# A fused long-convolution and gated-linear backward: net pace, fixed spectra homes, dW stores on another queue, four row blocks at once

## The chip, the core and the metric

One core of a Trainium2 chip runs the whole kernel in one launch. The metric is the device time of a launch in microseconds (us). The core has five engines, each with its own in-order instruction queue: TensorE (PE, matmuls), VectorE (DVE), ScalarE (ACT), GpSimd (POOL) and SyncE (SP). SP, ACT and POOL issue DMA transfers; an instruction that waits holds up everything behind it on its queue. Matmuls write to PSUM, which VectorE and ScalarE read out.

## The reference

The forward function takes the layer norm of x, multiplies a long convolution of it by a gated bilinear network, and adds x. The kernel returns its output and the gradients of everything but B_x. S = 2048 rows, D = 1024 columns, F = 3584; all tensors are bf16.

```python
xn = layernorm(x)                                 # x = A_q
k_shift = sum over t of k_pad[:, t:t+S] * shift_k[:, 3-t]
kv = k_shift * v
y = irfft(rfft(kv padded to 2S) * rfft(ssm_k padded to 2S))[:S] + kv * ssm_D
s = xn * y
h = (xn @ w_gate) * (xn @ w_up)
out = x + s * silu(h @ w_down)
_out, _vjp = jax.vjp(f, q, k, v, shift_k, ssm_k, ssm_D, w_gate, w_up, w_down)
return (out, *_vjp(grad_out))
```

## The kernel before

F is cut into 14 slabs of 256 columns (`NSL`), S into 16 row blocks of 128, D into 8 channel blocks (`ds`) of 128. The phases follow each other on TensorE; the two convolutions run beside them.

1. **Front end and gate/up** (0 to 562 us). The layer norm goes chunk by chunk over x (`ln_load`, `layer_norm`), the first two slabs of w_gate and w_up are multiplied as chunks come (`gu_unit`), and then the other slabs one after another. A tick is eight matmuls (L604). The products h are turned (`tr` L624, `hT`) and stored to HTd, Hd and GUd.
2. **Forward convolution**, beside it. `conv_forward` is a generator; `tick` calls a pump that advances it until its yielded units match the share of ticks that are done. Its spectra come from small DFT matmuls (`fwd4_half`, psF L232), whose results ACT copies and DVE combines. `shift` forms kv from k and v, which `load_kv` loads on POOL's queue, and `fwd4_half` reads kv. The spectra of kv and of ssm_k are stored to HFd and KFd.
3. **h @ w_down, gate and dbm** (562 to 755 us).
4. **dh and the weight gradients** (755 to 1379 us). Per slab `dw_slab` makes dW_gate and dW_up over eight `dc` steps (L1208), ACT casts each (L1213) into `wb` (three buffers, one per two steps), and two stores per `wb` go out on ACT's queue (`sta`). Between the steps `dh_half` computes dh of the next slab (L1191), DVE multiplies it into U, and SP stores that to DGd. `gu_in` and `load_wdt` load GUd and w_down, also on SP.
5. **Convolution backward**, beside it, pumped in the same way. `dy_forward` transforms dy (`fwd8_half`, psF; then `fwd8`) and stores DYFd; then 16 units multiply a spectrum A (DYFd) by a spectrum B (HFd or KFd), `product`, and transform back, `inv8` (psY L428).
6. **dW_down** (1379 to 1583 us): 14 steps `k`, each of two halves `f` (L1314); ACT casts into `wbs` (L1316, four buffers), SP stores it. Transposing DMAs on SP (`load_wgu` L1272 for the weights, `load_dgut` L1279 for the gradients of gate and up) run ahead for the next phase.
7. **dx** (1583 to 1991 us). dx_n is a sum over 14 pieces n, each a weight piece WGU[n] times a gradient piece dgut[n] of four row blocks (g); `dx_part` makes 8 matmuls (L1337) for one row block and n. Row blocks go in pairs; three PSUM tiles `psx` are in use. The layer norm's backward of a row block (`ln_backward`) loads dxna_t, xn_t and dout_t on SP, adds psx and dxna_t on DVE into `dxn`, and stores dx. Beside it run `dk_units` (dk and the shift gradients), 16 units paced by `kpump`, which load `kT` and `dkT` by transposing DMAs on SP and `dkh` on POOL.

What sets the order: the framework orders instructions on each engine by program order and priority, `tc.issue_after` holds an instruction behind another, and `high_priority` lifts one. `st` and `cld` issue on POOL's queue, `ld` on SP's, `sta` on ACT's. A tile of a pool waits until the last user of its buffer is done.

Of the kernel before, what the change touches and what calls it, by code (L numbers as in the profile page):

```python
# [19 lines left out]
def build_kernel(  # L20
# [217 lines left out]

    def fwd4_half(x, i, wp, psp, first=None):

        SP = wp.tile([P, 2, 2, 512], F32, name="SP", bufs=2)
        for par in range(2):
            ps = psp.tile([P, 2, 2, 256], F32, name="psF")
            cmm(ps[:, 0], T4[par], x, (i, i + 4), first if i == 0 else None, True)
            cmm(ps[:, 1], T4[par], x, (i + 2, i + 6))
            nc.scalar.copy(out=SP[:, :, par], in_=ps[:].rearrange("p s k x -> p s (k x)"))  # L246
        return SP
# [28 lines left out]
    def fwd8_half(x, i, wp, psp):  # L276

        SP = wp.tile([P, 2, 2, 512], F32, name="SP", bufs=2)
        for j in range(2):
            r = 2 * i + j  # L280
            ps = psp.tile([P, 2, 2, 256], F32, name="psF")
            cmm(ps[:, 0], T4[0], x, (r,))
            cmm(ps[:, 1], T4[0], x, (r + 4,))
            nc.scalar.copy(out=SP[:, :, j], in_=ps[:].rearrange("p s k x -> p s (k x)"))
        return SP
# [346 lines left out]
    def conv_forward():  # L632
# [39 lines left out]
        def h_rows(ds):  # L672
            hrow = S_.pop(("h", ds))
            hx = cs.tile([P, NB, P], BF16, name="hx")
            for c in range(2):
                ps = ps_tr.tile([P, 8, P], BF16, name="tr")
                with tc.issue_after(tr_ln[0].ins):
                    nc.tensor.transpose(ps[:, 0, :], hrow[:, c, :, 0], ident[:])
                for r in range(1, 8):
                    nc.tensor.transpose(ps[:, r, :], hrow[:, c, :, r], ident[:])  # L680
                nc.scalar.activation(hx[:, 8 * c:8 * c + 8, :], ps[:], ACT.Copy, scale=WSC)
            h_out.append(ds)
            if ds + 1 < 8:
                load_h(ds + 1)
            S_["hx"] = hx
# [4 lines left out]
        def tail(ds):  # L690
            G = S_.pop(("G", ds))
            yf = cs.tile([P, NB, P], BF16, name="yf")
            for rp in range(4):
                ps = inv_rows(G, ps_y, rp)
                nc.scalar.copy(out=by_res(yf[:], rp), in_=rowps(ps))
# [5 lines left out]
        load_kv(0, 0)  # L701
        load_kv(0, 1)
# [6 lines left out]
        for ds in range(8):  # L709
# [6 lines left out]
            yield 2.4  # L716
# [3 lines left out]
            yield 2.4  # L720
# [3 lines left out]
            yield 2.4  # L724
# [3 lines left out]
            yield 2.4  # L728
            W = fwd4_buf(cs)
            for i in range(2):  # L730
                fwd4_sums(W, sph[i], i)
                next(tl, None)
                yield 2.4
# [3 lines left out]
            for i in range(2):  # L737
                fwd4_outs(HX, W, i)
                next(tl, None)
                yield 2.4  # L740
# [21 lines left out]
    F_TOTAL = 4 * 20.0 + 6.0 + 8 * (0.5 + FWD4_W + 1.3 + PROD_W + INV_W) + 10.0  # L762
# [3 lines left out]
    ln_load(*xs[0])  # L766
    slabs = [load_slab(0, nc.sync)[0]]
    for c in xs[1:3]:
        ln_load(*c)
# [12 lines left out]
    last, root, xst = layer_norm(*xs[0])  # L782
    for i, (b0, n, x4) in enumerate(xs):
        if i + 1 < len(xs):
            with tc.issue_after(last.ins):
                last, root, xst = layer_norm(*xs[i + 1])
        for i_, sl in ([(i, 0), (i, 1)] if i < 4 else ([(4, 0)], [(5, 0), (4, 1), (5, 1)])[i - 4]):
# [86 lines left out]
    def dy_forward(cx, cs):  # L874
        def load(ds):
            if ds < 8:
                x = cx.tile([P, NB, P], BF16, name="dyx")
                cld(x[:], DYd[ds])
                xs_.append(x)
        xs_, sp = [], []  # L880

        def half(ds, i):
            if ds < 8:
                sp.append(fwd8_half(xs_[ds], i, cs, ps_c3))
# [5 lines left out]
        for ds in range(8):  # L890
            SPs = sp[2 * ds:2 * ds + 2]
            load(ds + 2)
            X = cs.tile([P, 16, 256], BF16, name="DX")
            yield from fwd8(SPs, X, cs, lambda i: half(ds + 1, i))
            st(DYFd[ds], X[:])

    def conv_backward():
        cx = pool("d_cx", 2)
        cs = pool("d_cs", 1)
        yield from dy_forward(cx, cs)  # L900
        ps_c3.release()
        ps_y4.append(pool("ps_y4", 4, space=PSUM))
        cs.release()
        cx.release()
        tfp.release()
        ab = pool("e_ab", 1)
        cs = pool("e_cs", 1)
        ew = pool("e_ew", 1)
# [3 lines left out]
        def load_a(n):  # L912
            if n < 16:
                As[n] = ab.tile([P, 16, 256], BF16, name="A", bufs=2)
                cld(As[n][:], DYFd[units[n][1]])

        def load_b(n):
            if n < 16:
                Bs[n] = ab.tile([P, 16, 256], BF16, name="B", bufs=2)
                cld(Bs[n][:], units[n][2][units[n][1]])  # L920
# [28 lines left out]
        PINQ[0] = False  # L949
        load_a(0)  # L950
        load_b(0)
        PINQ[0] = True
# [8 lines left out]
        ab.release()  # L961

# [241 lines left out]
    def dw_slab(sl, dgus, others):  # L1204
        for dc in range(DC):
# [123 lines left out]
    ps_x = pool("ps_x", 3, space=PSUM)  # L1329
# [136 lines left out]
```

## Time and profile before

Six runs took between 2002.84 and 2016.09 us, median 2007.62. The profiled execution is one of these.

| what | value |
|---|---|
| profiled execution, its own time | 2002.84 us |
| its span on the core | 2000.2 us |
| granted TensorE clock, mean | 0.992 |
| VectorE busy | 1512.6 us (76%) |
| ScalarE busy | 648.6 us (32%) |
| DMA traffic | 443.37 MB, mean 222 GB/s |
| packets under 512 B | 282624 of 455167 |
| matmuls, gate/up (L604) | 411.6 us, 1792 of 128x512 |
| matmuls, dW (L1208) | 397.2 us, 1792 of 128x512 |
| matmuls, dx (L1337) | 337.9 us busy for 1536 recorded |
| first dx matmul | 1591.38 us |
| last dx matmul | 1989.9 us |

Busy time is a share of the whole span and mixes phases with different limits. The wait lists give, for an engine, the line that waited, what released it, the total in us, how often, and the longest. The chain of waits, followed back from the last instruction, is on TensorE for 66% of the span, on DMA for 6% and on VectorE for 6%.

### The profile page before, as it was taken

What the parts mean: (1) busy time and instruction counts of PE and PEld (TensorE: products, weight loads), DVE (VectorE), ACT (ScalarE), POOL (GpSimd) and SP (SyncE); (2) the same over time, 40 slices, a digit from 0 to 9 for tenths busy, and PEclk for the clock granted to TensorE, in tenths of its full rate; (3) what the DMA queues carried; (4) which work ended last, traced back from release to release, by engine and by line L of the source; (5) the groups of instructions that cost most, each with busy time, mean ns of one, the idle gap of its engine ahead of it and who ended that gap; (6) DMA issues with size and microseconds to landing.
All of it is one profiled execution on the core that took longest, in us unless ns stands there. A gap on an engine that the chain in (4) does not pass through costs nothing.

```text
span 2000.2 us, 27457 instructions
## 1 busy us (share of the span) xinstructions
PE 1945.3 (97%) x11084; PEld 1044.2 (52%) x11084; DVE 1512.6 (76%) x1687; ACT 648.6 (32%) x954; POOL 331.6 (17%) x478
## 2 busy tenths in 40 slices
PE   7999999999999999999999999999999889999998
PEld 4455555555544446665566666654444334444443
DVE  7789999999636555888799999999976216666662
ACT  4765555545432224342222222222222101111112
POOL 3322213211212220000022121111212000101000
PEclk9999999999999999999999999999999999999999
DMA  8776766657799989664778898575998999696941
GB/s 287 241 265 223 252 205 228 202 178 250 255 286 295 296 268 286 210 217 171 253 238 280 207 262 268 196 279 180 210 244 184 150 222 202 149 205 145 210 113 57
DMA packets 455167, 443.37 MB, mean 222 GB/s; under 512 B 282624, under 2 KB 370488, under 8 KB 441216
## 3 DMA queue, kind: packets, MB, share of 16 engines
q1 hardware_dynamic: 367424, 226.83, 45.2%
q0 software_dynamic: 40832, 170.74, 26.3%
q10 hardware_dynamic: 46784, 44.05, 6.6%
q8 instruction: 86, 1.41, 0.3%
q14 instruction: 41, 0.34, 0.1%
HBM read 192.96 MB, written 189.83 MB: 191 GB/s over the span
## 4 chain that ended last, share of the span: by engine, by line
PE 66%; issue 15%; DVE 6%; DMA 6%; POOL 4%; SPq 2%; ACT 1%; POOLq 0%; DVEq 0%; ACTq 0%
PE psx L1337 17%; PE psb L1208 17%; PE psg L604 10%; PE psb L1314 8%; PE psb L1191 8%; PE psF L232 3%; DVE U L210 2%; SPq L1272 1%; DVE W L210 1%; DMA U<-Hd 1%; DMA KSLd<-in_A_k_dram 1%; PE psY L439 1%; DMA B<-HFd 1%; DMA dyx<-DYd 1%; PE psY L428 1%
## 5 line engine op out<-in xcount | busy, mean ns | idle before, releaser
L604 PE MATMUL psg<-wslab,U 128*128 128x512 bf16 x1792 | 411.6, 381 | 1.2 <-ACT U L570 1.1
L1208 PE MATMUL psb<-U,U 128*128 128x512 bf16 x1792 | 397.2, 379 | 0.0
L1337 PE MATMUL psx<-U,dgut 128*128 128x512 bf16 x1536 | 337.9, 382 | 15.4 <-DMA dgut<-DGd 7.8
L1337 PEld LDWEIGHTS <-dgut 128*128 128x128 bf16 x1792 | 175.7, 98 | 231.3 <-issue 12.6
L1208 PEld LDWEIGHTS <-U 128*128 128x128 bf16 x1792 | 175.2, 98 | 197.9
L604 PEld LDWEIGHTS <-U 128*128 128x128 bf16 x1792 | 173.5, 98 | 189.7 <-issue 6.3
L1191 PE MATMUL psb<-wdt,U 128*128 128x256 bf16 x1792 | 205.8, 273 | 1.1 <-ACT bm L1078 1.1
L1314 PE MATMUL psb<-U,U 128*128 128x512 bf16 x896 | 194.5, 379 | 1.8 <-DMA U<-Hd 1.8
L1191 PEld LDWEIGHTS <-U 128*128 128x128 bf16 x1792 | 175.3, 98 | 31.8 <-issue 1.4
L606 ACT CAST gut<-psg 128x512 bf16<-128x512 f32 x216 | 126.4, 586 | 180.5 <-PE psg L604 174.7
L1060 PE MATMUL psbm<-U,ht 128*128 128x512 bf16 x784 | 169.9, 379 | 0.0
L1213 ACT CAST wb<-psb 128x512 bf16<-128x512 f32 x112 | 65.6, 586 | 308.9 <-PE psb L1208 302.3
L210 DVE TENSOR_TENSOR W<-W 128x1024 f32<-128x1024 f32 (+1 forms) x144 | 142.5, 1008 | 2.9
L1314 PEld LDWEIGHTS <-U 128*128 128x128 bf16 x896 | 87.4, 98 | 106.6 <-DMA U<-Hd 2.3
L1360 ACT ACTIVATE dx_t<-dxn 128x1024 bf16<-128x1024 f32 (+1 forms) x17 | 17.1, 1007 | 334.2 <-DVE dxn L210 246.2
L1060 PEld LDWEIGHTS <-ht 128*128 128x128 bf16 x784 | 76.6, 98 | 91.8
L210 DVE TENSOR_TENSOR W<-SP 128x1024 f32<-128x1024 f32 x96 | 111.9, 1219 | 10.0 <-ACT SP L246 4.4
L1193 ACT CAST dht<-psb 128x512 bf16<-128x512 f32 x112 | 65.7, 587 | 119.1 <-PE psb L1191 113.0
L1039 DVE SCALAR_TENSOR_TENSOR dkp<-dkT,kT 128x1024 bf16<-128x1024 bf16 (+2 forms) x64 | 78.3, 1224 | 33.9 <-DMA dkT<-DKSHd 32.0
L210 DVE TENSOR_TENSOR U<-U,dht 128x2048 bf16<-128x2048 bf16 x56 | 68.3, 1221 | 44.6 <-ACT dht L1193 44.4
L210 DVE TENSOR_TENSOR m<-A,B 128x2048 bf16<-128x2048 bf16 (+1 forms) x48 | 73.1, 1575 | 31.2 <-DMA B<-HFd 16.7
L210 DVE TENSOR_TENSOR dxn<-psx,dxna_t 128x1024 f32<-128x1024 f32 (+1 forms) x17 | 19.7, 1161 | 97.6 <-DMA dxna_t<-DXNAd 63.5
(205 smaller groups left out, 2283.5 us busy)
## 6 DMA issues: line engine op xcount, KB each, us to landing
U<-GUd SPq DMA_DIRECT2D x28, 1024.0 KB, 8.1
DGd<-U SPq DMA_DIRECT2D x28, 1024.0 KB, 5.5
GUd<-gut ACTq DMA_DIRECT2D x54, 512.0 KB, 5.0
A<-DYFd POOLq DMA_DIRECT2D x16, 1024.0 KB, 8.8
out_dram<-wb ACTq DMA_DIRECT2D x112, 128.0 KB, 4.7
U<-Hd SPq DMA_DIRECT2D x14, 1024.0 KB, 6.6
Hd<-hN POOLq DMA_DIRECT2D x54, 256.0 KB, 4.3
HTd<-hT POOLq DMA_DIRECT2D x54, 256.0 KB, 3.2
```

The source lines that it names most:

```text
L210: pinned(V.tensor_tensor(o, a, b, op))
L232: mm = nc.tensor.matmul(ps[:, k].rearrange("p (c d) -> p c d", c=2), T[:, r, k, :], xr[:, r], start=(n == 0), stop=(n == len(rs) - 1 and ( ...
L604: gu_mm[0] = nc.tensor.matmul(ps[:], XNT[q][:, dc, qi * P:(qi + 1) * P], w[:, dc].rearrange("p a f -> p (a f)"), start=(dc == 0), stop=(dc ...
L606: nc.scalar.copy(out=gut[:, :, i], in_=ps[:].rearrange("p (a f) -> p a f", a=2))
L1039: ins = V.scalar_tensor_tensor(prod[:].rearrange("p r d -> p (r d)")[:, lo:H], dkT[:, 0, lo:H], 1.0, kT[:, 0, 13 + m + lo:13 + m + H], op0 ...
L1060: nc.tensor.matmul(ps[:, dh * 512:(dh + 1) * 512], ht(fc)[:, i * P:(i + 1) * P], WD[fc // 4][:, fc % 4, dh * 512:(dh + 1) * 512], start=(f ...
L1191: nc.tensor.matmul(ps[:, x * SLW:(x + 1) * SLW], DBMT[2 * hf + g][:, dc, (b % 4) * P:(b % 4 + 1) * P], wdt[:, dc, :], start=(dc == 0), sto ...
L1193: nc.scalar.copy(out=dht[:, 2 * e:2 * e + 2].rearrange("p b f -> p (b f)"), in_=ps[:])
L1208: nc.tensor.matmul(ps[:], XN[b // 4][:, b % 4, dc * P:(dc + 1) * P], dgus[b // 8][:, :, b % 8], start=(b == 0), stop=(b == NB - 1))
L1213: nc.scalar.copy(out=wb[:, dc % 2].rearrange("p a f -> p (a f)"), in_=ps[:])
L1314: nc.tensor.matmul(ps[:], h[:, b, f * P:(f + 1) * P], DBM[b // 4][:, b % 4, dh * 512:(dh + 1) * 512], start=(b == 0), stop=(b == NB - 1))
L1337: nc.tensor.matmul(ps[:, dh * 512:(dh + 1) * 512], t[n][:, f, i * P:(i + 1) * P], WGU[n][:, f, dh * 512:(dh + 1) * 512], start=(n == 0 and ...
```

## The change

Six edits are made together.

- The front end loads x's second chunk before the first slab, and the first k and v loads are held behind the store of the fifth chunk of xn (`xsts[4]`).
- The forward convolution counts the time its own matmuls take (`pe_us`), and `net` takes 0.95 of it off what a unit yields; F_TOTAL is lowered by the same sum.
- The convolution backward allots its buffers once: two homes for A (TF and A1), two for B. dy_forward's inputs and its DFT results live in A1, B0 and B1, and the first A and B are loaded in place of the half transforms that its last block has not.
- The dW_gate and dW_up stores move from ACT's queue to SP's.
- In the dW_down phase the transposing loads start one step later, and of the weight pieces 7 and of the gradient pieces 6 are issued there, not 9 and 9.
- In the dx phase four psx tiles are used. The first group g = 0 takes its four row blocks at once: for each n from 0 to 11 all four, then n = 12 and 13 for one row block after another with its ln_backward. The other groups are as before.

```diff
--- before.py
+++ after.py
@@ -236,8 +236,16 @@
             if first is not None and k == 0:
                 nc.tensor.matmul(ps[:, 0, 0:P], wsc_row[:], first, start=False, stop=True)
 
+    pe_us = [0.0]
+
+    def net(w):
+        w -= 0.95 * pe_us[0]
+        pe_us[0] = 0.0
+        return w
+
     def fwd4_half(x, i, wp, psp, first=None):
 
+        pe_us[0] += 1.75
         SP = wp.tile([P, 2, 2, 512], F32, name="SP", bufs=2)
         for par in range(2):
             ps = psp.tile([P, 2, 2, 256], F32, name="psF")
@@ -273,16 +281,14 @@
         if PIN[0]:
             tc.keep_in_program_order(ins)
 
-    def fwd8_half(x, i, wp, psp):
-
-        SP = wp.tile([P, 2, 2, 512], F32, name="SP", bufs=2)
+    def fwd8_half(x, i, SP, psp):
+
         for j in range(2):
             r = 2 * i + j
             ps = psp.tile([P, 2, 2, 256], F32, name="psF")
             cmm(ps[:, 0], T4[0], x, (r,))
             cmm(ps[:, 1], T4[0], x, (r + 4,))
             nc.scalar.copy(out=SP[:, :, j], in_=ps[:].rearrange("p s k x -> p s (k x)"))
-        return SP
 
     def fwd8(SPs, X, wp, ahead):
 
@@ -672,6 +678,7 @@
         def h_rows(ds):
             hrow = S_.pop(("h", ds))
             hx = cs.tile([P, NB, P], BF16, name="hx")
+            pe_us[0] += 0.95
             for c in range(2):
                 ps = ps_tr.tile([P, 8, P], BF16, name="tr")
                 with tc.issue_after(tr_ln[0].ins):
@@ -692,14 +699,16 @@
             yf = cs.tile([P, NB, P], BF16, name="yf")
             for rp in range(4):
                 ps = inv_rows(G, ps_y, rp)
+                pe_us[0] += 0.9
                 nc.scalar.copy(out=by_res(yf[:], rp), in_=rowps(ps))
                 if rp == 3:
                     st(YFd[:, :, ds * P:(ds + 1) * P], yf[:])
                 yield
 
         load_h(0)
-        load_kv(0, 0)
-        load_kv(0, 1)
+        with tc.issue_after(xsts[4].ins):
+            load_kv(0, 0)
+            load_kv(0, 1)
         yield from shift(0)
         PIN[0] = True
         yield 6.0
@@ -713,31 +722,31 @@
             W = fwd4_buf(cs)
             fwd4_sums(W, sp[0], 0)
-            yield 2.4
+            yield net(2.4)
...
@@ -759,14 +768,14 @@
         cs.release()
         cx.release()
 
-    F_TOTAL = 4 * 20.0 + 6.0 + 8 * (0.5 + FWD4_W + 1.3 + PROD_W + INV_W) + 10.0
+    F_TOTAL = 4 * 20.0 + 6.0 + 8 * (0.5 + FWD4_W + 1.3 + PROD_W + INV_W) + 10.0 - 0.95 * 8 * (4 * 1.75 + 0.95 + 4 * 0.9)
     chunks = [(0, 1), (1, 1), (2, 2), (4, 4), (8, 4), (12, 4)]
     xs = [(b0, n, u8((4, 6, 7)[b0 // 4 - 1], a=4) if n == 4 else lnp.tile([P, n, D], BF16, name=f"x{b0}")[:])
           for (b0, n) in chunks]
-    ln_load(*xs[0])
+    for c in xs[0:2]:
+        ln_load(*c)
     slabs = [load_slab(0, nc.sync)[0]]
-    for c in xs[1:3]:
-        ln_load(*c)
+    ln_load(*xs[2])
     slabs.append(load_slab(1, nc.sync)[0])
     for c in xs[3:]:
         ln_load(*c)
@@ -780,10 +789,12 @@
     bcast = load_bcast(bsb, ps_st)
     ang = angles(tg)
     last, root, xst = layer_norm(*xs[0])
+    xsts = [xst]
     for i, (b0, n, x4) in enumerate(xs):
         if i + 1 < len(xs):
             with tc.issue_after(last.ins):
                 last, root, xst = layer_norm(*xs[i + 1])
+            xsts.append(xst)
         for i_, sl in ([(i, 0), (i, 1)] if i < 4 else ([(4, 0)], [(5, 0), (4, 1), (5, 1)])[i - 4]):
             gu_unit(sl, *xs[i_][0:2], slabs[sl], nop)
             if i_ in (3, 4):
@@ -871,53 +882,46 @@
     ddo = const.tile([P, 8], BF16, name="ddo")
     dsko = const.tile([P, 8, 4], BF16, name="dsko")
 
-    def dy_forward(cx, cs):
+    def dy_forward(xs_, sp, cs, then):
         def load(ds):
             if ds < 8:
-                x = cx.tile([P, NB, P], BF16, name="dyx")
-                cld(x[:], DYd[ds])
-                xs_.append(x)
-        xs_, sp = [], []
+                cld(xs_[ds % 2], DYd[ds])
 
         def half(ds, i):
             if ds < 8:
-                sp.append(fwd8_half(xs_[ds], i, cs, ps_c3))
+                fwd8_half(xs_[ds % 2], i, sp[i], ps_c3)
+            else:
+                then[i]()
         load(0)
         load(1)
         yield 4.0
         half(0, 0)
         half(0, 1)
         for ds in range(8):
-            SPs = sp[2 * ds:2 * ds + 2]
             load(ds + 2)
             X = cs.tile([P, 16, 256], BF16, name="DX")
-            yield from fwd8(SPs, X, cs, lambda i: half(ds + 1, i))
+            yield from fwd8(sp, X, cs, lambda i: half(ds + 1, i))
             st(DYFd[ds], X[:])
 
     def conv_backward():
-        cx = pool("d_cx", 2)
+        ab = pool("e_ab", 1)
+        flat = lambda t, pat: t[:].rearrange(pat)
+        A_ = [flat(TF, "p a r k f -> p (a r k f)")] + [flat(ab.tile([P, 16, 256], BF16, name="A1"), "p a x -> p (a x)")]
+        B_ = [flat(ab.tile([P, 16, 256], BF16, name=f"B{i}"), "p a x -> p (a x)") for i in range(2)]
+        spec = lambda t: t.rearrange("p (a x) -> p a x", a=16)
         cs = pool("d_cs", 1)
-        yield from dy_forward(cx, cs)
-        ps_c3.release()
-        ps_y4.append(pool("ps_y4", 4, space=PSUM))
-        cs.release()
-        cx.release()
-        tfp.release()
-        ab = pool("e_ab", 1)
-        cs = pool("e_cs", 1)
-        ew = pool("e_ew", 1)
         units = [("v", ds, HFd) for ds in range(8)] + [("h", ds, KFd) for ds in range(8)]
         As, Bs, side_in = {}, {}, {}
 
         def load_a(n):
             if n < 16:
-                As[n] = ab.tile([P, 16, 256], BF16, name="A", bufs=2)
-                cld(As[n][:], DYFd[units[n][1]])
+                As[n] = spec(A_[n % 2])
+                cld(As[n], DYFd[units[n][1]])
 
         def load_b(n):
             if n < 16:
-                Bs[n] = ab.tile([P, 16, 256], BF16, name="B", bufs=2)
-                cld(Bs[n][:], units[n][2][units[n][1]])
+                Bs[n] = spec(B_[n % 2])
+                cld(Bs[n], units[n][2][units[n][1]])
 
         def load_side(n):
             kind, ds, _ = units[n]
@@ -946,10 +950,14 @@
                 return dkv_tail(ds, Bs[n], side_in.pop(n), ew)
             return dh_tail(ds, Bs[n], ew)
 
-        PINQ[0] = False
-        load_a(0)
-        load_b(0)
-        PINQ[0] = True
+        yield from dy_forward([A_[1][:, 2048 * i:2048 * i + 2048].rearrange("p (b d) -> p b d", b=NB) for i in range(2)],
+                              [b_.bitcast(F32).rearrange("p (s j x) -> p s j x", s=2, j=2) for b_ in B_], cs,
+                              (lambda: load_b(0), lambda: load_a(0)))
+        ps_c3.release()
+        ps_y4.append(pool("ps_y4", 4, space=PSUM))
+        cs.release()
+        cs = pool("e_cs", 1)
+        ew = pool("e_ew", 1)
         tl = None
         for n in range(16):
             yield from staggered(main(n), tl, 7.0)
@@ -959,6 +967,7 @@
         ew.release()
         cs.release()
         ab.release()
+        tfp.release()
 
     def dkv_tail(ds, G, tiles, ew):
         v, ksh = tiles
@@ -1214,7 +1223,7 @@
             if dc % 2 == 1:
                 fs, rows = slice(sl * SLW, (sl + 1) * SLW), slice((dc - 1) * P, (dc + 1) * P)
                 for a, dst in enumerate((o_dwg, o_dwu)):
-                    sta(dst[rows, fs].rearrange("(c p) f -> p c f", p=P), wb[:, :, a])
+                    ld(dst[rows, fs].rearrange("(c p) f -> p c f", p=P), wb[:, :, a])
             after_group(2)
             next(others, None)
 
@@ -1285,10 +1294,10 @@
         if k + 2 < NSL:
             load_h(k + 2)
         with tc.issue_after(wst.ins) if k > 0 else nullcontext():
-            if k in (1, 2, 3, 4, 5):
-                load_wgu(k - 1, u8((7, 0, 1, 9, 2)[k - 1], a=4))
-            if k in (6, 7, 8, 9):
-                ts.append(load_dgut(0, k - 6))
+            if k in (2, 3, 4, 5, 6):
+                load_wgu(k - 2, u8((7, 0, 1, 9, 2)[k - 2], a=4))
+            if k in (7, 8, 9, 10):
+                ts.append(load_dgut(0, k - 7))
         if k == 11:
 
             bdrain()
@@ -1296,15 +1305,12 @@
             tip.release()
             gw = pool("gw", 1)
             gd = pool("gd", 1)
-            for i in range(2):
-                load_wgu(5 + i, gw.tile([P, 4, D], BF16, name=f"W{i}")[:])
+            load_wgu(5, gw.tile([P, 4, D], BF16, name="W0")[:])
+        if k == 12:
+            load_wgu(6, gw.tile([P, 4, D], BF16, name="W1")[:])
             ts.append(load_dgut(0, 4))
-        if k == 12:
-            load_wgu(7, u8(6, a=4))
-            ts += [load_dgut(0, n) for n in (5, 6)]
         if k == 13:
-            load_wgu(8, u8(3, a=4))
-            ts += [load_dgut(0, n) for n in (7, 8)]
+            ts.append(load_dgut(0, 5))
         h = hs.pop(k)
         for f in range(2):
             wbs = wo.tile([P, D], BF16, name="wbs")[:]
@@ -1326,7 +1332,7 @@
     gl = pool("gl", 2, side="right")
     gs = pool("gs", 4, side="right")
     kw_ = pool("kw", 1)
-    ps_x = pool("ps_x", 3, space=PSUM)
+    ps_x = pool("ps_x", 4, space=PSUM)
     PIN[0] = True
     kpump, kdrain = make_pump(dk_units(kw_), DK_TOTAL)
     kcnt = [0]
@@ -1370,11 +1376,26 @@
             pinned(V.scalar_tensor_tensor(dx_t[:, cl], dxn[:, cl], RSTN[:, b:b + 1], dout_t[:, cl], op0=MUL, op1=ADD))
             (st if parts == 1 else ld)(out_1.flatten_outer_dims()[rows, cl], dx_t[:, cl])
 
-    for i, j in enumerate((11, 10, 8, 4, 5)):
+    for n in range(6, 14):
         with tc.issue_after(wst.ins):
-            load_wgu(9 + i, u8(j, a=4))
-            ts.append(load_dgut(0, 9 + i))
-    for g in range(4):
+            if n > 6:
+                load_wgu(n, u8((6, 3, 11, 10, 8, 4, 5)[n - 7], a=4))
+            ts.append(load_dgut(0, n))
+    pss = [ps_x.tile([P, D], F32, name="psx") for i in range(4)]
+    pss = pss[2:] + pss[:2]
+    for n in range(12):
+        for i in range(4):
+            dx_part(ts, i, pss[i], n)
+        ts[n] = load_dgut(1, n)
+    for i in range(4):
+        for n in (12, 13):
+            dx_part(ts, i, pss[i], n)
+        if i == 3:
+            for n in (12, 13):
+                ts[n] = load_dgut(1, n)
+        with tc.high_priority(40):
+            ln_backward(i, lambda h: pss[i][:])
+    for g in range(1, 4):
         for b in (4 * g, 4 * g + 2):
             if b == NB - 2:
                 break
```

More of the change, by code (lines that the diff above doesn't have):

```diff
@@ L719, in conv_forward @@
             sph = [fwd4_half(S_["hx"], 0, cs, ps_cv, D0)]
-            yield 2.4
+            yield net(2.4)
             KX = cx.tile([P, 16, 256], BF16, name="KX")
@@ L723, in conv_forward @@
             sph.append(fwd4_half(S_["hx"], 1, cs, ps_cv, D0))
-            yield 2.4
+            yield net(2.4)
             fwd4_outs(KX, W, 1)
@@ L727, in conv_forward @@
             next(tl, None)
-            yield 2.4
+            yield net(2.4)
             W = fwd4_buf(cs)
@@ L732, in conv_forward @@
                 next(tl, None)
-                yield 2.4
+                yield net(2.4)
             if ds < 7:
@@ L739, in conv_forward @@
                 next(tl, None)
-                yield 2.4
+                yield net(2.4)
             turned(HX, 1, 0, 1)
```

## The prediction

> **What bounds the kernel now.** I read the page's first part (busy us, share, instructions), then the list of waits of TensorE (PE), then the granted clock around each long wait, then the DMA-issuing queue of SyncE (SP).
>
> ```profile
> PE 1945.3 (97%) x11084; PEld 1044.2 (52%) x11084; DVE 1512.6 (76%) x1687; ACT 648.6 (32%) x954; POOL 331.6 (17%) x478
> ```
>
> TensorE is busy for 1945.3 of 2000.2 us, so all idle time is 54.9 us. No change that keeps the matmuls can win more, apart from matmuls that run slowly after a wait. The waits say where that time lies (total, times, longest):
>
> ```profile
> PE psx L1337 <- DMA dgut<-DGd: 7.8, 5, 3.1
> PE psx L1337 <- ACT wbs L1316: 7.6, 1, 7.6
> PE psF L232 <- DVE kv L210: 6.1, 3, 2.2
> PE psY L428 <- DVE B L272: 4.7, 2, 3.8
> PE tr L624 <- ACT hT L625: 4.2, 2, 3.1
> PE psb L1314 <- DMA U<-Hd: 1.8, 1, 1.8
> ```
>
> Rows 1 and 2 are at the start of the last phase, the others one each in the forward convolution, its backward, the front end and the dW_down phase. After some waits the clock drops, which the windows show (busy time of PE, PEld, DVE, ACT, POOL; then clock, DMA share, GB/s):
>
> ```profile
> 205.00:210.00 5.00, 4.72 (x28) 3.45 (x27) 4.96 (x5) 2.53 (x4) 2.80 (x4) 0.66 0.96 341
> 319.00:324.00 5.00, 4.50 (x38) 3.56 (x38) 4.96 (x5) 3.23 (x4) 1.71 (x3) 1.00 0.95 317
> 430.00:435.00 5.00, 4.60 (x26) 3.33 (x26) 4.96 (x5) 2.51 (x3) 1.38 (x3) 0.66 0.58 210
> 42.00:47.00 5.00, 5.00 (x31) 2.52 (x31) 2.46 (x8) 4.00 (x6) 4.83 (x7) 0.66 0.56 170
> 993.00:999.00 6.00, 4.11 (x20) 2.54 (x20) 5.96 (x8) 2.34 (x4) 0.00 (x0) 0.72 0.30 115
> 1591.00:1596.00 5.00, 4.62 (x13) 1.69 (x13) 4.66 (x7) 0.33 (x1) 0.00 (x0) 0.58 0.03 11
> ```
>
> A clock of 0.66 over 5 us is 0.34 x 5 = 1.7 us of work lost beside the wait.
>
> **Part by part, on the profiled run's clock (2002.84 us, 2.6 us around its span).**
>
> *Front end.* POOL issues in order. It waits for the KSLd copy (11.47 to 30.34, in the chain of waits), because load_kv's k load stands there; hT's stores stand behind it, and one starting at 34.43 takes 7.11 us to land. That gives the 3.05-us wait at 41.99 (row 5), then 1.7 us at the low clock. After, load_kv follows the fifth chunk's XNd store (49.46), so hT's stores go at once: 4.75 us gained. A later transposition then waits some 0.3 us longer (my estimate from 1.56 us at 49.22). k and v now land near 63 (issue 52 to 58, landing about 5 us); the shift's first product is at 64.13, so the cover is about 1 us, and if it is gone the DVE queue slips and PE with it later. Loading x's second chunk before slab 0 removes 0.53 us of DVE wait and delays slab 0 by about 0.4 us: nil. Take **-4.5** (-5 to 0).
>
> *Net pace.* The pump advances the convolution per tick of eight matmuls (1.73 us). F_TOTAL falls by 0.95 x 8 x 11.55 = 87.8 from 440.8 to 353.0 over 182.4 ticks, and the yields fall likewise, since PE's own convolution work already takes time. Units per tick go from (440.8-20)/182.4 = 2.31 to 1.83. The shift yields 20 plain units for its DVE work: 8.7 ticks before, 11.0 after, so its PE time grows from about 16.3 to 20.6 us. DVE needs 19.6 us plus 1.5 to 2 for the hN products mixed in, 21 in all: it was late by 2 to 4, and is then level. Row 3's waits (at 205.28, 319.49, 430.40; 1.97, 2.16, 1.97 us) go. How much more than 6.1 us is that? The Trainium skill ("TensorE: Matmul & The Clock Gate", "What's actually happening") puts the array at half clock after an idle window of about 3.4 us; none of these waits is that long, so by the rule they cost 6.1 and no more. The windows disagree: 0.66 after two of the three 2-us waits, 1.00 after the other. By the rows it is 6.1 + 2 x 1.7 = 9.5. I follow the rows, and leave a quarter because DVE is over 95% busy from 100 to 500 and can be late at another point. Take **-7** (-9.5 to +3: new waits of two us each at a few of 8 channel blocks).
>
> *Spectra.* DVE waited 16.7 us for B<-HFd (947.8 to 964.5): the load was issued at 949.15 behind A<-DYFd, after dy_forward's buffers were released. Now load_b(0) and load_a(0) are issued in the last fwd8, about 10 us sooner, into homes of their own; DVE's chain to psY moves up by at least the 4.75 us of row 4's waits, whose clock (0.72 over 6 us) costs 1.7 more. 6.4 at best. On the other side the first dyx load now shares A1 with a buffer that must be free first: issue moves from 767.67 to about 772, landing takes 8.8, PE reads it at 780.81: 0 to 1 us late, 6 if it lands as the second did (15.2). Take **-5** (-6.4 to +2).
>
> *dW stores.* 112 stores leave ACT's queue for SP's. ACT spent about 0.46 us of issue on each, 51 us, but its cast L1213 sat idle 302 us waiting for PE and PE has no wait between 1000 and 1550; nothing to gain. SP gets 8 more issues of about 0.5 us per 43-us slab. In the built order each pair stands at its natural place: after dc 1 before DGd, after dc 3 before wdt, after dc 5 behind the second DGd (SP waits there for DVE's product), after dc 7 between the GUd loads. wb has three buffers, 14 us or more of slack, and the waits between are below it. **0** (0 to +5).
>
> *dW_down and dx.* Before, the first row blocks go through dx two at a time, each n needing a transposed W (L1272) and dgut (L1279). SP's queue (start, us, what):
>
> ```profile
> 1573.59 6.73 SPq L1279 DMA_TRANSPOSE dgut<-DGd  x5
> 1582.85 4.46 SPq L1272 DMA_TRANSPOSE U<-in_B_w_up_dram  x1
> 1587.41 0.53 SPq L61 DMA_DIRECT2D out_dram<-wbs  x1
> ...
> 1632.85 4.51 SPq L1272 DMA_TRANSPOSE U<-in_B_w_gate_dram  x1
> 1637.41 2.65 SPq L1279 DMA_TRANSPOSE dgut<-DGd  x2
> 1640.10 4.68 SPq L1272 DMA_TRANSPOSE U<-in_B_w_up_dram  x1
> ...
> 1647.70 0.39 SPq L61 DMA_DIRECT2D dxna_t<-DXNAd  x1
> ```
>
> The stores of wbs stood behind transposes (SP was in L1279 and L1272 to 1587.31), so ACT's last cast had no buffer and the first psx matmul came at 1591.38, not 1583.8: 7.6 us, plus 0.42 x 5 = 2.1 for the clock. Later a pair of W and dgut comes every 7.25 to 7.5 us (1632.85 to 1640.10; 7.49 over four from 1610.14), while two row blocks use it up in 16 matmuls of 0.216 us: 3.46 us. The reserve of nine pairs runs out and PE waits 7.8 us, with 0.13 x 13 = 1.7 for the clock (0.87 from 1637 to 1650). Sum **19.2** us.
>
> After, four row blocks share each pair: 32 x 0.216 = 6.91 us per n. Fewer pairs are preloaded (7 W, 6 dgut), so the stores of wbs go out: row 2's wait goes. Row 6 stays (its order on SP is unchanged). I carry SP's queue forward with before's durations: kT of dk unit 0 at 1571, then units 1 to 3, each kT held by the taps of the unit before it (10.1 us a unit on DVE), dgut6 at 1607, seven pairs at 7.49: n = 13 is there at 1662 to 1665, and PE wants it at 1584.5 + 12 x 6.91 + 1.7 = 1669. No wait, by 4 us. PE ends the group at 1584.5 + 96.8 = 1681.3.
>
> **But the wait comes back.** All four PSUM tiles are taken. The next row block needs the first tile, which DVE frees with dxn, which needs dxna_t. In the built order SP issues dxna_t for block 0 only behind 14 transposed halves of the next group, for block 1 behind 10 more. One half takes 1.33 us (2.65 for two): 1663 + 18.6 = 1681.6 for the first, landed 3.5 us later, dxn done 1.2 after that: 1685.8, so PE waits 4.5. The second is issued at 1695.5, done at 1700.2; between lie 1.7 us of matmuls, so 12.7 more, with 1.7 for the clock: 18.9 us. Before, a third PSUM tile covered this, though DVE itself waited long for dxna_t (idle us, releaser at the end):
>
> ```profile
> L210 DVE TENSOR_TENSOR dxn<-psx,dxna_t 128x1024 f32<-128x1024 f32 (+1 forms) x17 | 19.7, 1161 | 97.6 <-DMA dxna_t<-DXNAd 63.5
> ```
>
> Net 19.2 - 18.9: **0** (-15 if SP is earlier than I carry it, +25 if later).
>
> Sum: -4.5 - 7 - 5 = -16.5; 2002.8 - 16.5 = 1986.3. The profiled run is 4.8 below the median of the runs shown (2007.62), so 1986.3 + 4.8 = **1991** as a median.
>
> **Rivals.**
> 1. *The dx group gains too.* SP's 24 halves go by before PE's end, as the dk units are short of what I take, or dxna_t is ready earlier: 1991 - 15 to 19 = **1974**. For it: a median half takes 1.30, and 4 us of reserve for the pairs may be more. Against: the taps of the dk units stand ahead of dgut6 in the order and hold SP to about 1607.
> 2. *The pace only moves the waits.* DVE, 95% busy from 100 to 500, is late elsewhere, and dyx lands late: 7 + 3 of the gain is lost: **2001**.
> 3. *Slower: SP's queue becomes the bound of dx.* Place: from dgut6 to dxna_t of block 1. Price: every us that SP is late there is a us of PE wait, once past the 4-us reserve for the pairs and at once for dxna_t. In the trace six halves took 11.78 us at 1682.09 beside two dk loads:
>
> ```profile
> 1682.09 11.78 SPq L1279 DMA_TRANSPOSE dgut<-DGd  x6
> ```
>
> 1.96 each. At that price 24 halves are 47 us rather than 32, 15 us more; one dk unit of 10.1 more makes 25: 1991 + 25 = **2016**. It decides from 22.6 us of lateness on (2013.6). Against: 8 halves at 1696.74 took 10.91, 1.36 each. A rule of the skill bears on it ("DMA: Bandwidth & Descriptors", "Issuing engines are not separate DMA queues"): issuing from several queues saves only the issuing time. By it, moving work to SP costs transfers nothing; the row says that a transpose holds SP itself 1.3 to 5.2 us, so a load behind 24 of them is late by 32. I take the row.
>
> **Numbers.** Forecast (1983 to 1999) 0.45; rival 1 0.16; rival 2 0.19; rival 3 0.20. What a measurement tells from no change is 0.3%, 6 us: 2001.6 to 2013.6. Faster: 0.45 + 0.16 + half of rival 2 less a little = 0.66. Same: the rest of rival 2 and the near end of rival 3, 0.16; slower 0.18. Range 1972 to 2014: from rival 1 with the bounds of the first parts to below rival 3.
>
> **What would show it.** TensorE's list without psF for kv, tr for hT above 1 us, psY for B above 1 us; psx no longer for ACT wbs or DMA dgut, but for DVE dxn, two waits of about 4.5 and 13 us near 1665 to 1690 (all earlier by the 16 us gained). dxna_t's first issue about at the end of the first group. Wrong if psx waits again for dgut within the first group, if psb waits in the dW slabs, or if a kv wait is still there.

## The result, and the profile after

The changed kernel took 1999.98 us (median of 29 runs, 1990.25 to 2015.96), the kernel before 2009.73 us (median of 66 runs, 1996.94 to 2022.35). The ratio is 0.9957, with an interval of 0.9943 to 0.9971: faster by 0.43%, or 8.6 us, about half of the 16.6 us that were forecast. The profiled execution of the changed kernel has a span of 1991.7 us and took 1993.8 us.

From TensorE's list of waits after the change, with the total, the times and the longest:

```profile
PE psx L1343 <- DVE dxn L210: 12.4, 1, 12.4
PE psx L1343 <- DMA dout_t<-in_grad_out_dram: 6.6, 1, 6.6
PE psF L232 <- DMA A<-DYd: 5.4, 1, 5.4
PE psx L1343 <- ACT wbs L1322: 0.7, 1, 0.7
PE psF L232 <- DVE kv L210: 0.6, 2, 0.4
```

Every wait that the prediction aimed at is gone or small: kv from 6.1 to 0.6 us, wbs from 7.6 to 0.7, the one of 3.1 us for hT is gone (4.2 us for hT in all before, 1.1 now), and neither dgut nor B is in the list. Three new waits stand at its head, 24.4 us together. The second row shows how a releaser can mislead: it names the load of dout_t, but the matmul went on at 1675.97, and DVE's dxn of row block 0, which had waited for dxna_t, ran from 1674.69 to 1675.92:

```profile
1674.69 1.23 DVE L210 TENSOR_TENSOR dxn<-psx,dxna_t 128x1024 f32<-128x1024 f32 x1 [75.74 <-DMA dxna_t<-DXNAd]
```

Both psx rows are waits for dxn.

SP's queue where they arise (start, us, what):

```profile
1647.96 22.77 SPq L1288 DMA_TRANSPOSE dgut<-DGd  x16
1670.97 0.39 SPq L61 DMA_DIRECT2D dxna_t<-DXNAd  x1
...
1672.40 15.26 SPq L1288 DMA_TRANSPOSE dgut<-DGd  x10
1687.76 0.53 SPq L61 DMA_DIRECT2D dxna_t<-DXNAd  x1
```

The load of dxna_t stands behind 16 transposed halves (the last two of the first group and 14 of the next), the following one behind 10 more. What the waits do to the clock is in the windows (busy PE, PEld, DVE, ACT, POOL; then clock, DMA share, GB/s):

```profile
1665.00:1670.00 5.00, 4.40 (x21) 1.89 (x20) 0.00 (x0) 0.00 (x0) 0.00 (x0) 1.00 1.05 192
1670.00:1675.00 5.00, 0.00 (x0) 0.00 (x0) 0.31 (x1) 0.00 (x0) 0.00 (x0) 0.66 0.97 237
1675.00:1680.00 5.00, 3.57 (x8) 1.13 (x8) 2.33 (x4) 3.54 (x5) 0.00 (x0) 0.50 1.05 219
1680.00:1690.00 10.00, 0.00 (x0) 0.00 (x0) 3.63 (x4) 0.00 (x0) 0.56 (x1) 0.50 1.09 207
1690.00:1695.00 5.00, 3.03 (x8) 1.08 (x8) 2.45 (x2) 2.27 (x4) 0.00 (x0) 0.50 1.18 227
```

The eight matmuls between the two waits and the eight behind the second run at 0.50. At 0.216 us each, 16 of them lose another 3.5 us.

To set stretches against each other I take when certain matmuls start, minus the same time in the kernel before. The third column is this pair of profiles. The fourth is the mean over all profiles in which that stretch's code is the changed kernel's, the experiments below included (6 to 10 of them).

| stretch | predicted | this profile | mean |
|---|---|---|---|
| start to the last bias row of the front end | -4.5 | -3.7 | -0.9 |
| to the last gate/up matmul | -7 | -7.2 | -7.1 |
| to the middle of the dW slabs | -5 | +0.9 | -2.0 |
| to the end of dW_down | 0 | -1.9 | -1.3 |
| dx | 0 | +3.4 | +8.0 |
| sum | -16.5 | -8.5 | -3.3 |

The mean sum from the profiled 2002.84 us of before is 1999.5, close to the measured median. That profile of before was a quick one: it lies 6.9 us below the median of all 66 runs, where the runs shown had made it 4.8. So the fourth column sets a mean against one quick profile, and it makes the change look worse than it is by up to these 6.9 us; in which stretch they lie is not known.

### The profile page after: what moved, and what is told of

It reads as the page before. It is cut to its first block, busy times and chain, and to the rows that moved or that the text cites. A ratio compares the mean times of both kernels' runs of the same rounds, so it can differ in the third digit from the quotient of the medians.

```text
span 1991.7 us, 27536 instructions
## 1 busy us (share of the span) xinstructions
PE 1938.6 (97%) x11084; PEld 1041.9 (52%) x11084; DVE 1511.3 (76%) x1687; ACT 648.0 (33%) x954; POOL 331.6 (17%) x478
## 3 DMA queue, kind: packets, MB, share of 16 engines
q0 software_dynamic: 40832, 170.74, 26.2%
## 4 chain that ended last, share of the span: by engine, by line
PE 76%; DVE 11%; issue 7%; DMA 2%; POOL 2%; SPq 1%; ACT 1%; POOLq 0%; DVEq 0%; ACTq 0%
PE psx L1343 19%; PE psb L1217 19%; PE psg L610 10%; PE psb L1320 10%; PE psb L1200 9%; PE psbm L1069 3%; PE psF L232 3%; DVE W L210 2%; DVE KX L210 2%; DVE U L210 2%; DVE HX L210 1%; DVE m L210 1%; SPq L1288 1%; PE psY L445 1%; DMA A<-DYd 1%
## 5 line engine op out<-in xcount | busy, mean ns | idle before, releaser
L1217 PE MATMUL psb<-U,U 128*128 128x512 bf16 x1792 | 397.2, 379 | 0.0
L1343 PE MATMUL psx<-U,dgut 128*128 128x512 bf16 x1536 | 336.9, 382 | 19.7 <-DVE dxn L210 12.4
L1217 PEld LDWEIGHTS <-U 128*128 128x128 bf16 x1792 | 175.2, 98 | 197.7
L1366 ACT ACTIVATE dx_t<-dxn 128x1024 bf16<-128x1024 f32 (+1 forms) x17 | 17.1, 1007 | 345.0 <-DVE dxn L210 297.0
L1322 ACT CAST wbs<-psb 128x512 bf16<-128x512 f32 x56 | 32.8, 586 | 159.6 <-PE psb L1320 149.1
L210 DVE TENSOR_TENSOR W<-SP 128x1024 f32<-128x1024 f32 x64 | 74.3, 1218 | 6.0 <-ACT SP L254 5.3
```

What stands on the lines that cost most here:

```text
L210: pinned(V.tensor_tensor(o, a, b, op))
L1217: nc.tensor.matmul(ps[:], XN[b // 4][:, b % 4, dc * P:(dc + 1) * P], dgus[b // 8][:, :, b % 8], start=(b == 0), stop=(b == NB - 1))
L1343: nc.tensor.matmul(ps[:, dh * 512:(dh + 1) * 512], t[n][:, f, i * P:(i + 1) * P], WGU[n][:, f, dh * 512:(dh + 1) * 512], start=(n == 0 and ...
```

## The experiments

Each is an edit of the changed kernel. Four of them ran 5 to 8 times, and their medians and ratios to the kernel before are given. The other six ran once each (1994.34, 2006.22, 2002.21, 1998.62, 1996.77 and 2004.73 us in the order below). The changed kernel's own runs span 26 us, so from these six only waits and stretches of the profile are read.

**A home of its own for dy_forward's first input.** A1 shares memory with a buffer that the last DBMd store and transposition still use.

```diff
+        cx = pool("d_cx", 1)
+        dyx0 = cx.tile([P, NB, P], BF16, name="dyx")
...
-        yield from dy_forward([A_[1][:, 2048 * i:2048 * i + 2048]...
+        yield from dy_forward([dyx0[:], A_[1][:, 0:2048]...
```

> The changed kernel, with a home of its own for dy_forward's first input, so that its load waits only for the stores of DYd. Theory A (the wait of 5.4 us at psF comes from the load being issued 4 us later, behind the transposes of wdt): the load goes out some 4 us sooner, lands in 7 to 9 us instead of 14.9, the psF wait falls below 1 us and the half pace behind it goes: 7 us gained, span 1984 to 1986. Theory B (what delays it is that both loads share the engines, whenever they start): landing stays at 13 us or more, the wait shrinks only by the 4 us of the issue, to 1 or 2 us, gain 4 to 5.

The load was issued at 758.59, when the last DYd store had landed and 3.0 us before the transposition, and landed in 9.0 us:

```profile
dyx<-DYd POOLq DMA_DIRECT2D x1, 512.0 KB, 9.0
```

No psF wait for it is left. From the last gate/up matmul to the second quarter of the dW slabs nothing is lost (-0.5 us; +7.3 in the changed kernel). No better time can be told: 2000.4 us as a median, ratio 0.9942 (0.9913 to 0.997), which overlaps the changed kernel's, and the span is 1992.5, not 1984 to 1986: TensorE began dx 3.4 us sooner, and the two psx waits were 22.3 us, not 19.0.

**The transposition moved, the loads left alone.**

```diff
-        if sl + 2 < NSL:
+        if 0 < sl < NSL - 2:
...
+                if sl == 0 and dc == 1:
+                    with tc.issue_after(wbst.ins):
+                        wdts.append(load_wdt(2))
```

> The changed kernel, with only the first w_down transpose of the dW slabs (the one at 759.7) placed behind the first pair of dW stores, some 11 us later. Theory A (transposes slow the dy loads): the loads, issued when they were, land in 7 to 10 us and the psF wait falls from 5.4 to 0 to 1 us. Theory B (the loads share with each other and with ordinary traffic): they still land in 13 to 15 us and the wait stays near 5.

DMA issues between 755 and 790 us, with the median time to landing at the end (of the three dy loads two go out together, a third later; in both kernels the median is the time of the first), first of the changed kernel:

```profile
A<-DYd POOLq DMA_DIRECT2D x3, 512.0 KB, 14.9
wdt<-in_B_w_down_dram SPq DMA_TRANSPOSE x1, 16.9
```

and of this one:

```profile
A<-DYd POOLq DMA_DIRECT2D x3, 512.0 KB, 6.6
wdt<-in_B_w_down_dram SPq DMA_TRANSPOSE x1, 4.8
```

The loads went out at the same place (760.94, against 760.61) and landed in 6.6 us instead of 14.9. The transposition itself fell from 16.9 to 4.8 us. So the transposition holds up the loads, and two loads side by side are not the reason. That the loads also hold up the transposition fits but is less sure, since it also moved away from two 1 MB stores of U. The psF wait is gone. In this one profile too the end of the kernel does not move: dx starts 6.0 us sooner than in the changed kernel and its waits for dxn are 23.2 us.

**dxna_t sooner.** It gets two buffers (`ln_a`), and the loads of row blocks 0 and 1 stand among the first reloads of dgut.

```diff
         for i in range(4):
             dx_part(ts, i, pss[i], n)
+        if n == 1:
+            pres.append((ln_a(0), ln_b(0)))
+        if n == 2:
+            pres.append((ln_a(1),))
         ts[n] = load_dgut(1, n)
```

> The changed kernel, with dxna_t in two buffers and the loads of row blocks 0 and 1 for ln_backward placed behind the second and third reload of dgut in the dx phase, not behind the seventh and twelfth. Theory A (PE waits for dxna_t, which stands behind 26 transposes on SP): both psx waits, 6.6 and 12.4 us, fall to under 1 us, and the 3.6 us of half pace go: 20 to 23 us gained, span 1969 to 1972. Rival (the transposes of group 1 themselves are late): the two waits go but psx then waits for dgut of group 1, 10 us or more, and the gain is under 12.

SP's queue in this kernel:

```profile
1655.19 0.39 SPq L61 DMA_DIRECT2D dxna_t<-DXNAd  x1
...
1659.86 0.58 SPq L61 DMA_DIRECT2D dxna_t<-DXNAd  x1
1660.53 28.10 SPq L1288 DMA_TRANSPOSE dgut<-DGd  x20
```

and its psx waits, apart from 0.7 us for wbs:

```profile
PE psx L1343 <- DMA dgut<-DGd: 3.5, 5, 1.3
```

PE runs through from the first row group into the second, so the cause of the two waits is shown. 1991.8 us as a median, ratio 0.9899 (0.9866 to 0.9931), which does not overlap the changed kernel's 0.9943 to 0.9971: between the ratios lie 0.58%, some 12 us. The 3.5 us for dgut lie in groups 2 and 3, after 1788.

The profile is that of the quickest of the eight runs, and its gain is in two parts. From the end of dW_down to the last dx matmul it gains 15.0 us on the kernel before, where the changed kernel loses 3.4. That makes 18.4 us, and 20.5 with what lies ahead of dx. But the span, 1981.5 us, is only 10.2 us shorter than the changed kernel's, and not the 1969 to 1972 expected. From the start of the last dx matmul to the end it takes 20.1 us here and 9.9 there, because TensorE is no longer what ends last:

```profile
1955.78 5.99 PE L1343 MATMUL psx<-U,dgut 128*128 128x512 bf16 x27
1967.78 0.69 DVE L210 TENSOR_TENSOR dxn<-psx,dxna_t 128x512 f32<-128x512 f32 x1
```

The last product is done at 1961.77 and DVE takes it up 6 us later. The chain of waits, followed back from the end, runs over DVE's layer norm and dk units and SP's queue and meets psx only at 1667; in the changed kernel it is psx up to 1982. After 1780 DVE had waited for xn_t, which still has one buffer and whose loads stand behind dgut, here and in the changed kernel:

```profile
DVE prod L210 <- DMA xn_t<-XNd: 25.9, 2, 14.2
DVE prod L210 <- DMA xn_t<-XNd: 5.2, 2, 3.2
```

No run moves xn_t as well, so it is not shown that this wait is what holds the end.

**The old dx phase.** Parts of the dW_down loads and the first row group as in the kernel before.

```diff
-    ps_x = pool("ps_x", 4, space=PSUM)
+    ps_x = pool("ps_x", 3, space=PSUM)
...
-    for g in range(1, 4):
+    for g in range(4):
```

> The changed kernel, with the dW_down phase's loads and the dx phase as before (three psx tiles, pairs, nine pairs of pieces preloaded). Theory A (the four-block group gave back what it saved): time within 3 us of the changed kernel, psx waiting again for ACT wbs and DMA dgut, 15 us in all, and psb for Hd about 1.8. Rival (the first group's part is a gain that something else ate): 10 us or more slower than the changed kernel.

```profile
PE psx L1346 <- DMA dgut<-DGd: 7.1, 4, 2.8
PE psx L1346 <- ACT wbs L1325: 6.9, 1, 6.9
PE psx L1346 <- DVE dxn L210: 3.2, 2, 1.8
```

The waits removed by the change are back, and in this run DVE's dxn adds 3.2 us that the profile of before did not have. Its dx stretch is 3.9 us longer than in that profile, with the same code. 1995.69 us as a median of 5 runs, ratio 0.9934 (0.9886 to 0.9983), which overlaps the changed kernel's interval. The four-block group as it stands is worth nothing that these runs can tell, and the rival, that it gains 10 us or more, falls.

**The pace as before.**

```diff
     def net(w):
-        w -= 0.95 * pe_us[0]
...
-    F_TOTAL = ... + 10.0 - 0.95 * 8 * (4 * 1.75 + 0.95 + 4 * 0.9)
+    F_TOTAL = ... + 10.0
```

> The changed kernel with the forward convolution's pace as before (nothing taken off its units, F_TOTAL 440.8). Theory (the pace removes the three waits of psF for kv and the half clock behind them): the three waits are back, 1.9 to 2.2 us each, 6 us in all, and the stretch from the last bias row of the front end to the last gate/up matmul is 6 to 9 us longer than in the changed kernel. Rival (the waits went because k and v come from another place in POOL's queue): no wait for kv above 0.5 us, and the stretch is the same within 2 us.

```profile
PE psF L232 <- DVE kv L210: 6.1, 3, 2.2
```

The same three waits, to a tenth, and the clock behind them is as before: 0.66, 1.00 and 0.66 over 5 us. From the bias row to the end of gate/up it is as long as before the change (0.0 us), 7.1 longer than with the pace.

**k and v loads where they stood.**

```diff
-        with tc.issue_after(xsts[4].ins):
-            load_kv(0, 0)
-            load_kv(0, 1)
+        load_kv(0, 0)
+        load_kv(0, 1)
```

> The changed kernel with the first k and v loads where they stood before. Theory (the k load blocked hT's stores on POOL): a wait of tr for ACT hT of 2.5 to 3.5 us near 39 to 42 us is back with the low clock behind it, so the front end's last bias row is 3 to 5 us later, while DVE's wait of 6.2 us for k near 65 is gone. Rival (the move gave nothing: what is saved on hT is lost on late k): the last gate/up matmul stands within 2 us of the changed kernel's other runs (548.6 to 551.0).

The wait for hT is back (2.9 us the longest) and DVE's 6.2-us wait for k near 65 us is gone. The bias row stands at +0.1, against a mean of -0.9 and values of -3.7 to +1.2 with the move, and the last gate/up matmul at 550.9, inside the span of the others (546.7 to 551.6). In this one profile both mechanisms are there, and what is left of the gain is below what the front end varies by from run to run.

**k and v loads 12 us sooner.** The same hold, on `xsts[3]`.

> The changed kernel with the first k and v loads behind the fourth chunk's xn store, not the fifth's, about 12 us sooner. If late k costs something: DVE's wait for k (6.2 us at 65) falls to under 2, tr does not wait over 1.5 us for hT, and the last gate/up matmul is 2 to 3 us earlier than the mean of the runs with the same pace (549.5). If late k is hidden: no difference beyond 2 us, as the clock in the first 100 us varies more than that.

DVE waits 4.0 us there, for something that the profile does not name; the last k load had been issued at 43. The last gate/up matmul is at 546.0, 3.5 us before the stated mean and 0.7 before the changed kernel's own profile. One profile is not enough to call it a gain, since the front end varied by 5 us in the runs above.

**Both mends.** dxna_t sooner and the transposition later.

> The changed kernel with both mends: dxna_t of row blocks 0 and 1 early (two buffers), and the first w_down transpose of the dW slabs behind the first pair of dW stores. If the two costs are independent: dy waits and dxn waits both gone, about 22 + 5 us less than the changed kernel, 1974 to 1981 as a median, ratio to the kernel before 0.981 to 0.987. If the first group's pairs become late as everything upstream is earlier (the margin was 4 us): psx waits for dgut in the first group by 2 to 6 us, and the ratio is 0.986 to 0.990.

1988.84 us as a median, ratio 0.9886 (0.986 to 0.9913): quicker than the changed kernel and the one before, but not to be told from dxna_t alone. The ratio is the one expected for late pairs, but the place is another. In the profiled execution of this kernel (1995.07 us, the slowest of its six) the first group waited 0.8 us for dgut, and groups 2 and 3 waited 10.3, such as at 1794:

```profile
1794.00 44.19 PE L1346 MATMUL psx<-U,dgut 128*128 128x512 bf16 x192 [4.51 <-DMA dgut<-DGd]
```

with SP's queue before it:

```profile
1770.85 12.14 SPq L1291 DMA_TRANSPOSE dgut<-DGd  x6
1783.09 1.25 SPq L1020 DMA_TRANSPOSE kT<-in_A_k_dram  x1
1784.39 1.29 SPq L1022 DMA_TRANSPOSE dkT<-DKSHd  x1
1785.77 12.57 SPq L1291 DMA_TRANSPOSE dgut<-DGd  x6
```

Six halves in 12.1 and in 12.6 us, 2.0 to 2.1 each, beside DVE's dk units and their loads. Group 2's dgut has to be reloaded within the 48 us of group 1's second pair, and 28 halves at 2 us are 56. Why these loads were slower here is open: dx began only 0.8 us sooner than with dxna_t alone, whose profile, the quickest of eight, waited 3.5 us for dgut. The end is again not TensorE's: 17.1 us lie behind the start of the last dx matmul.

**The convolution backward's buffers as before.**

```diff
-        A_ = [flat(TF, ...)] + [flat(ab.tile(..., name="A1"), ...)]
+                As[n] = ab.tile([P, 16, 256], BF16, name="A", bufs=2)
```

> The changed kernel with the convolution backward's buffers as before (dy_forward's inputs in a pool of their own, A and B allotted after it). Theory (the fixed homes win 6.4 us at psY and lose 1 to 7 us at the first dy load): psY waits again for DVE B, 4.7 us, DVE m for B<-HFd about 16 us, and the first dyx load, issued 4 us after the last DYd store, lands in 7 to 9 us, so psF waits under 1 us for it. From the last gate/up matmul to the end of the dW slabs it is 0 to 6 us longer than in the runs with fixed homes. Rival (the dy wait comes from the stores of dW on SP's queue): psF waits for dyx 3 us or more here too.

```profile
PE psY L436 <- DVE B L280: 1.9, 2, 0.9
```

DVE waits 13.9 us for B<-HFd, and psF has no wait for dyx, as expected. But psY waits only 1.9 us, not 4.7. From the last gate/up matmul to the middle of the dW slabs this kernel gains 4.4 us on the kernel before, more than the mean with fixed homes (2.0). Of that stretch, the part behind the first quarter of the slabs gains 6.4 us in every profile with fixed homes and 3.9 here; the homes lose it again ahead of that, at the first dy load. So the homes, with the late dy load they bring, were no gain in these runs. With that load mended, as in three of the kernels above, the stretch gains 6.8 us, 2.5 more than here. Why the old buffers stall less here than in the kernel before was not tried.

**dW stores back on ACT's queue.**

```diff
-                    ld(dst[rows, fs].rearrange("(c p) f -> p c f", p=P), wb[:, :, a])
+                    sta(dst[rows, fs].rearrange("(c p) f -> p c f", p=P), wb[:, :, a])
```

> The changed kernel with the dW stores on ACT's queue as before. Theory (they cost and gain nothing on either queue): no wait of psb at L1217 on either, and the dW slabs, from their second quarter to their end, last within 1 us of the changed kernel's. Rival (the stores on SP delay its loads): the first dy load or GUd's loads land sooner, and the slabs are 2 us or more shorter.

psb at L1217 waits in neither kernel. The dW slabs lost 4.5 us in their second half, with one wait of 2.6 us for ACT's dht at 1142.7, while ACT had waited 11.8 us for a DGd store. The kernel before has its stores on ACT as well and no such wait, so one profile does not say whether the queue is the cause; it stays open.

## Why the prediction was right in kind and wrong in size

The measured 1999.98 us lies in the stated range and on the forecast side, but the gain is about half the one forecast: 8.6 us by the ratio and 9.8 between the medians, against 16.6. The mechanisms were the ones named. Three terms of the sum had the wrong size: the new wait in dx, the first dy load and the front end.

*The pace* was right in mechanism and size: -7.1 measured in ten profiles (-6.8 to -7.2), -7 predicted, and undoing it brings back the three waits and all of it. In the size there is some luck. The waits that went are 5.5 us (6.1 less the 0.6 left), and 1.6 more was gained: nearer to the 6.1 of the rule that the prediction quotes than to the 9.5 of its rows. The -7 came from taking a quarter off for new waits behind a busy DVE, which did not come (DVE was 93 to 97% busy there, not over 95 throughout). The low clock after two of the three waits is real, as it came back with them; why it did not cost the whole 3.4 us is not shown.

*The new wait in dx* was right in place, order and cause. In the changed kernel n = 13 was loaded at 1651, and the group ended at 1669.4; the prediction's times, less the 11.9 us gained before it, are 1650 to 1653 and 1669.4. **What failed is the size of the wait, "so PE waits 4.5" and "with 1.7 for the clock: 18.9 us", and with it "Net 19.2 - 18.9: 0".** The first dxna_t was to be issued 97.1 us after the first dx matmul. It was 98.4 in the changed kernel's profile and 101.0 to 104.0 in the seven others with this dx phase. Two terms were short. "One half takes 1.33 us": 16 halves took 22.77 us and 10 took 15.26, 1.42 and 1.53 each, 3.4 us more in all. And the stretch of pairs, from dgut6 to the long run of halves, took 54.3 us in this profile but 55.8 to 59.0 in the others. So the first wait was 6.6 us here and 9.2 to 10.9 elsewhere, not 4.5; the second, 12.4 to 13.8, was close to the 12.7 predicted. The price of the clock was 3.5 us, not 1.7, as both waits halve it. With the clock that makes 22.5 us here and 26.2 in the mean of eight profiles, where 18.9 stood. Against the 19.2 saved it leaves +3.3 and +7.0; the table has +3.4 and +8.0. (The sum 1681.6 + 3.5 + 1.2 is 1686.3, not 1685.8; this shifts 0.5 us from one wait to the other.)

Are gains upstream taken back in dx, because SP's queue keeps its own time? The two experiments on the dy wait look like it: dx began 3.4 and 6.0 us sooner than in the changed kernel, the waits were longer by 3.3 and 4.2 us, and the spans are 1992.5 and 1991.6 against 1991.7. But the eight profiles with this dx phase do not bear it out. The first dx matmul stands between 1566.5 and 1578.8, the last between 1981.5 and 1994.0, and the late starters end late. SP moves up too: dgut6 is issued 20.9 to 22.3 us after the first dx matmul in all eight. It is the changed kernel's profile that was quick in dx, 409.3 us from the first matmul to the last where the other seven took 413.2 to 415.4. So a gain of some 5 us upstream is neither shown to be lost nor, by the overlapping ratios, shown to be kept.

*The first dy load*, "0 to 1 us late, 6 if it lands as the second did", failed in its choice. The other half of that sum held: behind the first quarter of the slabs 6.4 us are gained, as predicted. The trace of before held the answer on the load: the first one was issued at 767.67, before the transposition at 770.60, and the one that took 15.2 us after it, at 771.65. Four microseconds' delay moved the first load to the other side. Besides, no view gives the 8.8 us for the first load; the completions recorded for it end at 778.95, 11.3 us after its issue, and from 772 on these alone would have made it 2.5 us late. The wait was 1.3 to 6.0 us in the seven profiles with this order, and gone in all four without it. The stretch with the fixed homes gained 2.0 us in the mean, not 5.

*The front end* was right about the blocked queue and missed in its sum: -0.9 in the mean, not -4.5. The 3.05-us wait for hT is gone, and k came late as the 1-us cover suggested (DVE waited 6.2 us for it). The granted clock over the first 100 us went from 0.95 to 1.00 among profiles of the same front-end code, and each 0.01 there is at most 1 us. One pair of profiles cannot carry a claim of 4.5 us there.

*Smaller points.* The 1.8-us wait for Hd, which I kept, was gone in this profile and came back at 0.4 to 2.3 us in others. dW stores: no psb wait at L1217, as predicted. The rival of a slower SP queue had the right mechanism; 38 us for 26 halves is a fifth of the way from its 1.33 to its 1.96 us each, and not enough to make the kernel slower.

## What to carry to other kernels

When a change removes the bound of a stage, follow each queue to the instruction that frees the next buffer, and carry that queue forward with the times of a busy stretch, not with the best ones. Put the small load that releases a buffer ahead of a long run of prefetches, not where the program text happens to have it: that reordering was worth some 12 us here. Then look again at what ends last: in that profile TensorE's last matmul came 20 us sooner and the end of the kernel 10, as DVE had become the last. Before a load is moved by a few microseconds, look at what is issued on the other queues between the old and the new place. And do not explain the difference of two profiles before you know by how much profiles of the same code differ.

## What the runs showed of the hardware that was not expected

- A transposing load of w_down and two plain 512 KB loads on another queue, in flight together, took 16.9 and 14.9 us to land (the first of the two loads); apart, 4.8 and 6.6.
- Two waits of 6.6 and 12.4 us, with only eight matmuls between them, held the clock at 0.50 from 1675 to 1695: the short burst did not bring it back.
- Kernels with the same front end were granted 0.95 to 1.00 of the clock over the first 100 us; the cause is open.
- Waits of only 2 us were followed by a clock of 0.66 over 5 us in two of three places, before the change and again with the pace undone.
